# Two heads in natural rows per row group, and the shifted chord of VectorE's exponential on GpSimd

## The chip, the cores and the metric

One core of one Trainium2 chip runs the whole program. The metric is the device time of one execution in microseconds (us), as the median of the runs named. A run more than 1.5% above the fastest of its kernel is called slow and left out of the ratios. Every version was run beside the kernel before, on the same chip in the same session, and the ratio of their fast runs is given with its 95% interval; two changed versions may have run on different chips, so they are compared through these ratios, and differences of their medians are rough. The granted clock is the clock that TensorE was given, as a share of full speed.

## The reference

Attention with 32 heads of width 16 over 2048 positions, then a layer norm with a residual, then a SwiGLU feed-forward block. Cut to what matters:

```python
B, S, D, H, F = 1, 2048, 512, 32, 1792
q, k, v = split(x @ wqkv)                        # 32 heads, Dh = 16
scores = einsum("bhqd,bhkd->bhqk", q, k) * Dh ** -0.5
p = softmax(scores)                              # 32 * 2048 * 2048 exponentials
attn = einsum("bhqk,bhkd->bhqd", p, v)
... attn @ wo, layer norms, residual ...
h = silu(x @ w1) * (x @ w3);  out = h @ w2
```

The exponentials are the load: 1024 score tiles of 128x1024. The rest has to fit beside them.

## The kernel before

The kernel is written as a planner: the program's own scheduler simulates the engines when the program is built and fixes the order of instructions on each engine. The order is then executed as it stands; only semaphores move things in time.

Each score tile goes to ScalarE, which takes a true exponential, or to VectorE, which builds one from integer operations on pairs of tiles:

```python
# VectorE: y = scores as int16 in a fixed-point log2 scale, read from PSUM twice per pair
tensor_scalar(y, ps, G_LO, 32767.0, ALU.max, ALU.min)          # PSUM read, 128x1024, twice
# then on the pair, 128x2048:
tensor_scalar(m, y, 0x7F, 0x3F00, ALU.bitwise_and, ALU.bitwise_or)   # mantissa
tensor_scalar(g, y, -G_LO, 0.0, ALU.add, ALU.max)                    # shifted chord
tensor_tensor(m, y.bitcast(BF16), m.bitcast(BF16), ALU.mult)         # product
tensor_scalar(y, y, 0x7F80, None, ALU.bitwise_and)                   # exponent, in place
```

The results (product, chord, exponent) are three terms that TensorE adds up: each VectorE tile costs three products with V ("PV") in place of one. They live in a few buffers.

```python
NY = 3        # y, and the exponent, which is written in place
NM = 2        # mantissa and product
NG_ = 2       # chord
```

A switched-off path could already give the chord to GpSimd, in another form than VectorE's (the y of this kernel is clamped by the PSUM read, so the max with 0 is not needed):

```python
POOL_G = False
...
# on GpSimd, if POOL_G:
tensor_scalar(g, y, -G_LO, 1.0, ALU.add, ALU.mult)
```

Heads lie at every second group of 16 rows, with a constant row between them that adds the exponent bias; K and Q are brought there by strided moves, and GpSimd prepares the constant rows with seven fills.

## Time and profile before

| | before |
|---|---|
| median of 4 runs | 814.25 us (812.09 to 815.43) |
| span of the profiled run | 812.3 us |
| busy: TensorE, VectorE, ScalarE, GpSimd | 775.6, 775.1, 776.0, 44.1 us |
| first score; first exponential on VectorE | 18.6; 48.9 us |
| last exponential; tail after it | near 795; 17.3 us (cut at 795) |
| tiles on ScalarE and VectorE | 794 and 230 |

The prediction below shows the lines these are from. In a line of the costliest groups, the part before the first bar says what ran, then come busy time in us and the mean ns of one, then the idle time of that engine just before the group and who ended it. "PE ps L..." as releaser is a TensorE instruction of that source line.

### The profile page before, as it was taken

The numbers are of one execution on the slowest core, as the hardware profiler recorded it, in microseconds if no ns is written. First come the engines' busy times: TensorE is split into PE (matmuls) and PEld (weight loads), VectorE is DVE, ScalarE is ACT, GpSimd is POOL, SyncE is SP. The second block draws the span as 40 slices with busy tenths as digits, with TensorE's granted clock in tenths as the row PEclk, the third lists the DMA queues.
The fourth block names the chain that finished last, engine by engine and source line by source line (L and its number), as shares of the span: only waits on it lengthen the run. The fifth ranks groups of instructions, "written<-read, shape, count | busy, mean of one in ns | idle before, by whom it ended". The sixth has DMA issues, their size and how long they took to land.

```text
span 812.3 us, 20816 instructions
## 1 busy us (share of the span) xinstructions
PE 775.6 (95%) x8925; PEld 224.6 (28%) x8925; DVE 775.1 (95%) x1015; ACT 776.0 (96%) x874; POOL 44.1 (5%) x54
## 2 busy tenths in 40 slices
PE   6999999999999999999999999999999999999987
PEld 4332222222222222222222222222222222222222
DVE  8679999999999999999999999999999999999982
ACT  4899999999999999999999999999999999999992
POOL 4500100000000000000001000000000000000000
PEclk9999999999999999999999999999999999999997
DMA  5216333233222313333112434321223432222211
GB/s 182 54 31 149 49 49 52 45 54 40 29 22 41 49 38 43 41 54 47 19 25 28 60 41 54 48 33 40 18 27 55 67 34 34 49 27 22 28 9 31
DMA packets 88783, 36.96 MB, mean 45 GB/s; under 512 B 73193, under 2 KB 85097, under 8 KB 88681
## 3 DMA queue, kind: packets, MB, share of 16 engines
q1 hardware_dynamic: 88680, 35.53, 29.9%
q8 instruction: 72, 1.18, 0.6%
q14 instruction: 31, 0.25, 0.1%
HBM read 22.81 MB, written 2.10 MB: 31 GB/s over the span
## 4 chain that ended last, share of the span: by engine, by line
ACT 50%; PE 24%; DVE 19%; DMA 3%; issue 2%; POOL 1%; SPq 1%; DVEq 0%; POOLq 0%
ACT f_PT L1788 48%; PE ps L1356 9%; PE ps L1742 8%; DVE f_xd L1837 6%; PE ps L2010 6%; ACT f_th L1517 3%; DVE f_xd L1900 3%; DVE f_xd L1909 2%; DVE f_xd L1950 2%; DVE f_xd L1893 2%; DMA f_R<-f_Rrow 2%; DMA f_Rrow<-f_Rc 1%; DVE f_hT L1531 1%; SPq L2058 1%; DVE f_t L1521 1%
## 5 line engine op out<-in xcount | busy, mean ns | idle before, releaser
L1788 ACT ACTIVATE f_PT<-ps 128x1024 bf16<-128x1024 f32 x794 | 746.4, 1091 | 9.9 <-PE ps L1742 9.1
L1742 PE MATMUL ps<-f_QT,f_KT 32*128 32x512 bf16 x2048 | 331.0, 385 | 14.1 <-ACT f_PT L1788 7.1
L1837 DVE TENSOR_SCALAR f_xd<-ps 128x1024 int16<-128x1024 f32 x230 | 278.6, 1211 | 1.6 <-PE ps L1742 1.2
L2010 PE MATMUL ps<-f_PT,f_Vaug 128*17 128x512 bf16 (+1 forms) x1588 | 211.0, 386 | 0.3 <-DVE f_xd L1900 0.3
L2010 PE MATMUL ps<-f_xd,f_Vaug 128*17 128x512 bf16 (+1 forms) x1380 | 191.5, 387 | 3.5 <-DVE f_xd L1950 2.6
L1742 PEld LDWEIGHTS ps<-f_QT,f_KT 32*128 32x128 bf16 x2048 | 83.5, 91 | 328.6 <-ACT f_PT L1788 277.2
L1356 PE MATMUL ps<-f_xnT,f_w 128*32 128x512 bf16 x1792 | 145.0, 384 | 2.5 <-DVE f_hT L1531 0.9
L1900 DVE TENSOR_TENSOR f_xd<-f_xd 128x2048 bf16<-128x2048 bf16 x115 | 142.1, 1235 | 0.0
L1909 DVE TENSOR_SCALAR f_xd<-f_xd 128x2048 int16<-128x2048 int16 x115 | 81.2, 706 | 0.0
L1893 DVE TENSOR_SCALAR f_xd<-f_xd 128x2048 int16<-128x2048 int16 x115 | 79.4, 691 | 0.6 <-PE ps L1356 0.2
L1950 DVE TENSOR_SCALAR f_xd<-f_xd 128x2048 int16<-128x2048 int16 x115 | 79.0, 687 | 0.0
L1356 PE MATMUL ps<-f_w,f_hT 128*32 128x512 bf16 x896 | 74.9, 384 | 0.0
L2010 PEld LDWEIGHTS ps<-f_PT,f_Vaug 128*17 128x17 bf16 (+1 forms) x1588 | 50.6, 92 | 54.4 <-issue 44.7
L2010 PEld LDWEIGHTS ps<-f_xd,f_Vaug 128*17 128x17 bf16 (+1 forms) x1380 | 46.2, 92 | 54.7 <-issue 30.4
L2075 POOL TENSOR_TENSOR f_onorm<-f_U,f_R 128x512 bf16<-128x512 f32 x15 | 21.5, 1431 | 705.2 <-DMA f_R<-f_Rrow 549.3
L1356 PEld LDWEIGHTS ps<-f_xnT,f_w 128*32 128x32 bf16 x1792 | 36.6, 94 | 64.9 <-issue 56.5
L1517 ACT ACTIVATE f_th<-ps 128x512 f32<-128x512 f32 x56 | 38.7, 691 | 0.0
L1531 DVE SCALAR_TENSOR_TENSOR f_hT<-f_t,ps 128x512 bf16<-128x512 bf16 x56 | 37.8, 675 | 0.7 <-PE ps L1356 0.5
L1521 DVE SCALAR_TENSOR_TENSOR f_t<-f_th,ps 128x512 bf16<-128x512 f32 x56 | 37.7, 674 | 0.5 <-ACT f_th L1517 0.3
L1356 PEld LDWEIGHTS ps<-f_w,f_hT 128*32 128x32 bf16 x896 | 18.6, 94 | 26.8 <-issue 22.4
L1356 PE MATMUL ps<-f_wo,f_onorm 128*32 128x512 bf16 x272 | 22.2, 401 | 1.9 <-POOL f_onorm L2075 1.8
L2028 DVE COPY f_U<-ps 128x512 f32<-128x512 f32 x31 | 21.1, 679 | 0.4 <-PE ps L2010 0.3
(80 smaller groups left out, 240.6 us busy)
## 6 DMA issues: line engine op xcount, KB each, us to landing
f_w<-in_B_w_dram SPq DMA_DIRECT2D x112, 128.0 KB, 2.7
f_R<-f_Rrow SPq DMA_DIRECT2D x124, 32.0 KB, 4.4
f_xr<-in_A_x_dram SPq DMA_DIRECT2D x16, 128.0 KB, 3.8
out_dram<-f_xn_sb SPq DMA_DIRECT2D x16, 128.0 KB, 2.5
f_KT<-f_stg SPq DMA_DIRECT2D x31, 64.0 KB, 2.0
f_QT<-f_stg SPq DMA_DIRECT2D x31, 64.0 KB, 2.0
f_U<-f_U SPq DMA_DIRECT2D x60, 32.0 KB, 1.9
f_w<-in_B_w_dram SPq DMA_DIRECT2D x7, 256.0 KB
```

The source lines that it names most:

```text
L1356: ins = e.matmul(bank(bk)[32 * i:32 * i + 32, 0:ncols], make_lhsT(i), rhs_ap, start=start, stop=stop, tile_position=(0, 32 * i))
L1517: q = P.op("act", lambda e: e.activation(th[:, ss, :], bank(bk), ACTF.Tanh, scale=0.5), reads=[("ps", bk)], writes=[("th", ss)], dur=a_cos ...
L1521: q2 = P.op("dve", lambda e: e.scalar_tensor_tensor(t1[:, ss, :], th[:, ss, :], 1.0, bank(bk), ALU.add, ALU.mult), reads=[("th", ss), ("ps ...
L1531: q = P.op("dve", lambda e: e.scalar_tensor_tensor(hT[:, fc, :], t1[:, ss, :], 0.5, bank(bk), ALU.mult, ALU.mult), reads=[("t1", ss), ("ps ...
L1742: ins = e.matmul(bank(b), l_, r_, start=True, stop=True, tile_position=(rp, 0))
L1788: q = P.op("act", lambda e: e.activation(PT[:, s_, :], ps[:, b0 * 512:(b0 + 2) * 512], ACTF.Exp, scale=ASC, bias=ABIAS), reads=[("ps", b0) ...
L1837: q = P.op("dve", lambda e: e.tensor_scalar(dsl[:, ys, 1024 * c:1024 * c + 1024], ps[:, 4 * 512:6 * 512], G_LO, 32767.0, ALU.max, ALU.min) ...
L1893: P.op("dve", lambda e: e.tensor_scalar(dsl[:, NY + m_, 0:n], y, 0x7F, 0x3F00, ALU.bitwise_and, ALU.bitwise_or), reads=YK, writes=[("ds", ...
L1900: q_ = P.op("dve", lambda e: e.tensor_tensor(t_ap.bitcast(BF16), y.bitcast(BF16), t_ap.bitcast(BF16), ALU.mult), reads=YK + [("ds", NY + m ...
L1909: q_ = P.op("dve", lambda e: e.tensor_scalar(g_ap, y, -G_LO, 0.0, ALU.add, ALU.max), reads=YK, writes=[("g", g_, k) for k in range(n // 51 ...
L1950: q_ = P.op("dve", lambda e: e.tensor_scalar(y, y, 0x7F80, None, ALU.bitwise_and), reads=YK, writes=YK, dur=s_cost(n), name="e", lock=True)
L2010: ins = e.matmul(bank(PV)[32 * j:32 * j + (17 if g % 2 == 0 else 32), :], v_, p_, start=s0, stop=s1, tile_position=(0, 32 * j))
```

## The change

The intent is to relieve VectorE twice: to take the chord from it, in pieces of 128x1024 on the idle GpSimd, each released beside a PSUM read because such a read and GpSimd leave each other alone (1.22 and 1.27 us side by side, in the prediction's lines); and to start earlier. Two heads lie in natural rows of a row group, and Q is masked to one of them, so the strided moves and fills vanish. The core of the diff, with cuts:

```diff
-    POOL_G = False
+    NE = 2
+    E_WAIT = 6.0
+    G_POOL = 1.05
+    E_LAG = 0.8
 ...
-                q = ... tensor_scalar(dsl[:, ys, ...], ps[:, 4 * 512:6 * 512], G_LO, 32767.0, ALU.max, ALU.min)
-                beside(q, 1024)
+                before = P.ops["dve"][-1]
+                q = ... tensor_scalar(dsl[:, ys, ...], ps[:, 4 * 512:6 * 512], YB, G_LO, ALU.add, ALU.max)
+                if eq and P.free["pool"] <= P.t + 0.15 and eq[0][1]() is not None:
+                    it = eq.pop(0)
+                    it[2](it[3], before)          # a piece on GpSimd, waiting for `before` alone
 ...
-                q_ = P.op("pool", lambda e: e.tensor_scalar(g_ap, y[:, c0:c0 + w], -G_LO, 1.0, ALU.add, ALU.mult), ...
+            def p_g(c, after, eng="pool"):
+                q_ = P.op(eng, lambda e: e.tensor_scalar(g_ap[:, cs], y[:, cs], -G_LO, 0.0, ALU.add, ALU.max),
+                          ..., dur=G_POOL if eng == "pool" else s_cost(1024), name="g", ...)
 ...
-                q_ = ... tensor_scalar(y, y, 0x7F80, None, ALU.bitwise_and)       # exponent in place
+                q_ = ... tensor_scalar(e_ap, y, 0x7F80, None, ALU.bitwise_and)    # exponent in its own buffer
 ...
+                if eq and P.t - eq[0][0] > E_WAIT and ...:
+                    it[2](it[3], None, "dve")     # a piece that waited 6 us goes back to VectorE
 ...
-        for g in range(1, NG):
-            P.post("pool", lambda g=g: kt_fill(g), ...)        # and stg, pad, pack: strided moves
+                    q = ... tensor_scalar(QT[:, s0, :], QT[:, s1, :], msk[:, 0:1], None, ALU.mult)
+                    q = ... tensor_scalar(QT[:, s1, :], QT[:, s1, :], msk[:, 1:2], None, ALU.mult)
```

## The prediction

> **What bounds the kernel now.** I read the page's busy shares and slices first, then the costliest groups, then busy time by stage, then timelines of a few microseconds in the steady part and around the GpSimd instructions.
>
> ```profile
> PE 775.6 (95%) x8925; PEld 224.6 (28%) x8925; DVE 775.1 (95%) x1015; ACT 776.0 (96%) x874; POOL 44.1 (5%) x54
> ...
> PE   6999999999999999999999999999999999999987
> PEld 4332222222222222222222222222222222222222
> DVE  8679999999999999999999999999999999999982
> ACT  4899999999999999999999999999999999999992
> POOL 4500100000000000000001000000000000000000
> ```
> Three engines are full together from the third slice to the last but one; GpSimd has nothing to do. The 5% that is missing lies at the two ends.
>
> ```profile
> L1788 ACT ACTIVATE f_PT<-ps 128x1024 bf16<-128x1024 f32 x794 | 746.4, 1091 | 9.9 <-PE ps L1742 9.1
> L1742 PE MATMUL ps<-f_QT,f_KT 32*128 32x512 bf16 x2048 | 331.0, 385 | 14.1 <-ACT f_PT L1788 7.1
> L1837 DVE TENSOR_SCALAR f_xd<-ps 128x1024 int16<-128x1024 f32 x230 | 278.6, 1211 | 1.6 <-PE ps L1742 1.2
> ...
> L1900 DVE TENSOR_TENSOR f_xd<-f_xd 128x2048 bf16<-128x2048 bf16 x115 | 142.1, 1235 | 0.0
> L1909 DVE TENSOR_SCALAR f_xd<-f_xd 128x2048 int16<-128x2048 int16 x115 | 81.2, 706 | 0.0
> L1893 DVE TENSOR_SCALAR f_xd<-f_xd 128x2048 int16<-128x2048 int16 x115 | 79.4, 691 | 0.6 <-PE ps L1356 0.2
> ...
> L1950 DVE TENSOR_SCALAR f_xd<-f_xd 128x2048 int16<-128x2048 int16 x115 | 79.0, 687 | 0.0
> ```
> Softmax has 1024 score tiles of 128x1024. ScalarE takes the exponential of 794; VectorE takes 230, in 115 pairs: two PSUM reads, then mantissa, shifted chord (L1909), product, exponent. The schedule is fixed when the program is built and gives a tile to whichever engine is free, so a tile saved on one engine is shared out. The two engines end together, and this balance is what the change moves.
>
> The groups' means contain the pipeline's tail, so for throughput I use start to start distances of the timeline: PSUM read 1.14 us (97.89 to 99.03), product 1.13 (432.14 to 433.27), chain operation 0.60 (96.69 to 97.29), 512-wide PSUM evacuation 0.60, exponential 0.917 (a run of 7 in 6.42 us in the chain of work).
>
> ```profile
> 0.00:18.60 18.60, 11.47 (x104) 8.03 (x104) 14.82 (x39) 7.51 (x11) 8.56 (x20) 1.00 0.63 198
> ...
> 18.60:48.90 30.30, 28.40 (x444) 11.87 (x444) 19.91 (x40) 26.24 (x34) 11.48 (x12) 1.00 0.16 37
> 48.90:795.00 746.10, 724.00 (x8242) 199.65 (x8238) 737.35 (x928) 738.78 (x827) 24.05 (x22) 1.00 0.31 42
> ```
> Columns: stretch, length, then busy us of PE, PEld, DVE, ACT, POOL. The first score comes at 18.6 us. VectorE starts on exponentials only at 48.9 and was idle for 10 of the 30 us before. The last exponential ends near 795; a tail of 17 us follows.
>
> **What the skill says, and whether the trace agrees.**
> "SBUF — State Buffer", section "Who interferes with whom": GpSimd shares a port pair with VectorE as an exclusive lock; a VectorE instruction in a two-port mode, or with two SBUF inputs against a GpSimd read, collides and the later one waits out the earlier; one with at most one SBUF input outside those modes does not. The trace agrees both ways:
>
> ```profile
> 7.82 1.90 POOL L1275 TENSOR_SCALAR f_KT<-f_pat 128x2048 int16<-128x2048 int16 x1
> 7.88 2.30 DVE L1242 TENSOR_SCALAR f_xn_sb<-f_xd,f_mv,f_lnr 128x512 bf16<-128x512 bf16 x2 [0.59 <-POOL f_lnr L1230]
> ...
> 97.89 1.22 DVE L1837 TENSOR_SCALAR f_xd<-ps 128x1024 int16<-128x1024 f32 x1
> ...
> 98.10 1.27 POOL L2075 TENSOR_TENSOR f_onorm<-f_U,f_R 128x512 bf16<-128x512 f32 x1 [62.30 <-DVE f_xd L1909]
> ...
> 432.33 2.75 POOL L2075 TENSOR_TENSOR f_onorm<-f_U,f_R 128x512 bf16<-128x512 f32 x1 [48.12 <-DVE f_xd L1837]
> ```
> Two normalisations behind a GpSimd fill took 2.30 us, where two take 0.70 elsewhere. The PSUM read at 97.89 kept its 1.22 us beside GpSimd, and GpSimd its 1.27; at 432.33, beside the product, GpSimd took 2.75. So PSUM reads are the right hiding place, and the only large one.
> "GPSIMD Engine Reference", section "Engine selection": one-input elementwise work runs at roughly line rate. The seven GpSimd fills agree: 1.90 us for 2048 int16, 1.05 for 1024 f32, so I take 1.05 us for a 1024-wide chord (an estimate: the fills read a broadcast column, not a full tile).
> "TensorEngine Tiling (Array Packing)", section "Key Properties": changing the tiling mode drains the array. At 301 us a step between a score and a column group takes 0.32 us, between two column groups 0.22.
>
> **The change, part by part.**
> 1. Chord to GpSimd. Each pair loses one 0.60 us operation on VectorE: from 2 x 1.14 + 1.13 + 3 x 0.60 = 5.21 us to 4.61, or 2.60 to 2.30 us per tile. GpSimd gets two pieces of 1.05 us per pair, about 125 x 2.1 = 260 us in all, which it has free.
> 2. What the lock takes back. A piece is released by the end of the instruction ahead of the PSUM read. That end comes 0.08 us into the read (1.22 long, 1.14 apart), and a VectorE to GpSimd signal takes 0.09 (5.28 to 5.37 us). So the piece ends about 0.08 + 0.09 + 1.05 = 1.22 us into the read, while the next VectorE instruction is due at 1.14. If that is a chain operation it waits 0.1 us or a little more: per pair up to 0.2, per tile 0.1. I take 2.40 us per tile.
> 3. Natural rows. Gone are the strided moves of K and Q, GpSimd's seven fills, ScalarE's two fills and the second computation of the first K and Q tiles. The constant row becomes the add of the PSUM read (add and max in place of max and min: same cost). Added: two masked copies of Q per Q tile, 15 x 2 x about 0.25 = 7 us of VectorE (estimated from the 0.35 us normalisation of the same width).
> 4. Start-up. K and Q of the first rows are made in 128-column pieces as each transposed tile arrives, and the collision at 7.88 us (1.6 us of the starting chain) goes: first score near 15 us instead of 18.6. Three quarters of V move out of the early part, and K no longer waits for fills and moves, so VectorE's exponentials start near 33 us instead of 48.9. The V evacuations then fall into the steady part: 16 x 0.47 us, half on each engine, 4 us each.
>
> Balance before. ScalarE: 19.1 + 794 x 0.917 (728) + 56 tanh x 0.48 (27) + early evacuations and gaps (21, the remainder) = 795. VectorE: 48.9 + 230 x 2.60 (598) + other work 128 (112 SwiGLU, 31 U, 27 K/Q and 30 output evacuations at 0.60, small ones 8) + gaps 16 (the remainder) = 791. The sums meet, so the model stands.
> Balance after, with n tiles on VectorE. ScalarE: 15 + 17 + 27 + (1024 - n) x 0.917 = 998 - 0.917 n. VectorE: 33 + 2.40 n + 128 + 7 + 4 + 16 = 188 + 2.40 n. Equal at n = 244, ending at 774 us instead of 795. With no lock loss it is n = 252 and 767; with twice the loss n = 237 and 781. The tail stays: 774 + 17 = 791 of span, and the timed runs lie 1 to 2 us above it: 793.
> By parts: with 2.60 us per tile kept, the balance gives n = 230 and 787, so of the 21 us about 8 are the start-up (masks paid) and 13 the offload.
>
> **Rivals.**
> A. TensorE becomes the bound. It is busy 724.0 of 746.1 us, and most of its small gaps are mode switches, not waits. Every tile on VectorE needs three PV products in place of one: 14 more tiles are 14 x 0.22 = 3 us more. Against it: a score of VectorE mostly rides behind one of ScalarE, so a tile fewer on ScalarE saves a visit to score mode (0.64 - 0.22 = 0.42 us), 6 us in all. TensorE's need from first score to last exponential stays near 750 us (28.4 + 724.0 before) in a stretch of 759. It fits barely. If it does not, feed-forward work is left for the tail: 800 to 806.
> B. The lock costs more. If the chord needs 1.3 us on a full tile, or pieces slip behind the product, each PSUM read loses 0.3 us or more, the 0.60 us saved is spent, and only the start-up gain is left: 787 + 17 + 2, about 805. Against: the pieces wait for the instruction ahead of the read, and the schedule sends late ones back to VectorE after 6 us.
> C. The start-up gain is swallowed, because TensorE is already busy 28.4 of 30.3 us there: 4 to 6 us less gain, about 798.
> D. The integer conversion does not saturate. The kernel tests this and would then run its slow path as well: far above 1000 us. I give it 1%.
>
> **Range and chances.** 2% is 16.3 us, so the line is 797.2. The offload alone would not pass it, nor the start-up alone; together they do with 4 us to spare. Rivals A to C each take 5 to 12 us, all from the same side; no lock loss and a shorter tail give back 7 to 10. I say 793, 781 to 806, faster 0.62, same 0.35, slower 0.03.
>
> **What would show it.** Step 1: the mantissa and exponent groups grow to about 120 pairs, the chord group leaves VectorE, GpSimd near 300 us busy, about 240 PSUM reads and 780 exponentials. Step 2: GpSimd pieces near 1.05 us, PSUM reads still 1.21, chain operations behind them 0.1 us longer in the mean. Step 4: first score near 15 us, first VectorE exponential near 33. A: ScalarE shows gaps released by scores, and feed-forward tiles stand after the last exponential. B: chain or product means well above 0.8 and 1.35 us. The prediction is wrong if VectorE's tiles stay near 230, or if ScalarE's last exponential ends after 785.

## The result, and the profile after

The changed kernel takes 974.04 us (median of 4 runs, 967.61 to 985.35) against 814.25; its result is right. One of the four runs was slow (985.35 us at a granted clock of 0.889; the others had 0.907 to 0.909). The ratio is 1.194, with an interval of 1.187 to 1.201. All ratios in this document are the mean time of one kernel's fast runs over that of the other's of the same rounds, so not quite the ratio of the medians that are quoted.

The page of the profiled execution (967.61 us): busy time, and the 40 slices.

```profile
PE 842.5 (87%) x9201; PEld 228.8 (24%) x9201; DVE 810.9 (84%) x1013; ACT 787.4 (82%) x866; POOL 648.7 (67%) x209
...
PE   8898998879889998889989998789888888879887
...
DVE  8888998887869798878989897898987888978872
ACT  6888898878779797778889997798986878868880
POOL 3565785687666696776846775777778975969510
PEclk9979899988879799888989999899987979988999
```

No engine is full any more: three stand at 82 to 87% all along, where they were at 95%. GpSimd, which was to be busy for about 300 us, is busy for 649. The last row is new too: the granted clock of TensorE is below 0.9 in 17 of the 40 slices and 0.907 in the mean, against 0.992 before (its busy time grew from 776 to 843 us with about the same work).

The costliest groups of the kernel after:

```profile
L1817 ACT ACTIVATE f_PT<-ps 128x1024 bf16<-128x1024 f32 x790 | 755.1, 1040 | 146.6 <-PE ps L1771 130.4 <-PE ps L2027 13.6
L1964 POOL TENSOR_SCALAR f_xd<-f_xd 128x1024 int16<-128x1024 int16 x164 | 616.1, 3772 | 249.8 <-DVE f_xd L1922 147.6 <-DVE f_hT L1556 28.2 <-DVE f_xd L1940 21.1
L1868 DVE TENSOR_SCALAR f_xd<-ps 128x1024 int16<-128x1024 f32 x234 | 284.0, 1214 | 32.0 <-PE ps L1771 31.2
...
L2027 PE MATMUL ps<-f_xd,f_Vaug 128*17 128x512 bf16 (+1 forms) x1404 | 206.5, 415 | 72.0 <-POOL f_xd L1964 63.2 <-DVE f_U L2045 3.9 <-DVE f_t L1546 1.8
...
L1929 DVE TENSOR_TENSOR f_xd<-f_xd 128x2048 bf16<-128x2048 bf16 x117 | 152.9, 1307 | 0.0
L1940 DVE TENSOR_SCALAR f_xd<-f_xd 128x2048 int16<-128x2048 int16 x117 | 98.7, 843 | 5.0 <-PE ps L2027 5.0
```

The chain of work that ended last, followed back through the whole execution, as the page of each kernel gives it: first the kernel after, then the kernel before.

```profile
PE 35%; POOL 28%; DVE 21%; issue 7%; ACT 4%; DMA 3%; SPq 1%; DVEq 0%; POOLq 0%
ACT 50%; PE 24%; DVE 19%; DMA 3%; issue 2%; POOL 1%; SPq 1%; DVEq 0%; POOLq 0%
```

GpSimd, which was in 1% of that chain, is now in 28% of it.

The second line of the groups carries the result: one piece on GpSimd takes 3.77 us in the mean, not 1.05. The lines around it show what comes of that. TensorE's products with V stood idle for 63 us until GpSimd had finished (L2027), ScalarE stood idle for 130 us until TensorE made a score (L1771), and VectorE's product and exponent operation grew from 1.24 and 0.69 us to 1.31 and 0.84.

The same kernel by stages; the columns are the stretch, its length, then the busy us of TensorE, its weight loads, VectorE, ScalarE and GpSimd, and the granted clock. The stretches are cut at the first score, the first exponential on VectorE and the last exponential.

```profile
11.60:31.80 20.20, 18.73 (x440) 9.88 (x444) 16.78 (x46) 18.64 (x24) 4.53 (x10) 1.00 0.24 59
31.80:938.00 906.20, 792.92 (x8284) 200.04 (x8284) 778.65 (x928) 760.85 (x831) 639.29 (x183) 0.90 0.23 31
938.00:966.00 28.00, 21.76 (x359) 10.49 (x357) 6.80 (x15) 3.02 (x5) 0.00 (x0) 0.95 0.11 33
```

So the start gained what was hoped for and more: the first score comes at 11.6 us instead of 18.6, VectorE's first exponential at 31.8 instead of 48.9. The steady stretch lost it all many times over: 906 us instead of 746. The tail grew by 11.

A few microseconds of the timeline after (start, length, what ran, and in brackets the idle time before it and who ended that):

```profile
297.11 7.79 POOL L1964 TENSOR_SCALAR f_xd<-f_xd 128x1024 int16<-128x1024 int16 x2
...
299.53 0.69 DVE L1922 TENSOR_SCALAR f_xd<-f_xd 128x2048 int16<-128x2048 int16 x1 [1.72 <-PE ps L2027]
...
301.35 0.40 PE L2027 MATMUL ps<-f_xd,f_Vaug 128*32 128x512 bf16 x4 [1.08 <-POOL f_xd L1964]
...
302.12 4.69 ACT L1817 ACTIVATE f_PT<-ps 128x1024 bf16<-128x1024 f32 x5 [1.04 <-PE ps L1771]
```

This is the chain in small. A first piece runs on GpSimd from 297.11 to about 301; TensorE waits 1.08 us for it; the next score is late by that; ScalarE waits 1.04 us for the score. But look at the second line also: a mantissa operation of VectorE, one of the kind that needs the shared ports, ran in its usual 0.69 us in the middle of the slow piece. So the piece does not keep the ports for its whole length.

### The profile page after: what moved, and what is told of

Its sections match the earlier page's. It is cut to its first block, busy times and chain, and to the rows that moved or that the text cites. A ratio compares the mean times of both kernels' runs of the same rounds, so it can differ in the third digit from the quotient of the medians.

```text
span 965.5 us, 21581 instructions
## 1 busy us (share of the span) xinstructions
PE 842.5 (87%) x9201; PEld 228.8 (24%) x9201; DVE 810.9 (84%) x1013; ACT 787.4 (82%) x866; POOL 648.7 (67%) x209
## 3 DMA queue, kind: packets, MB, share of 16 engines
q8 instruction: 74, 1.21, 0.5%
## 4 chain that ended last, share of the span: by engine, by line
PE 35%; POOL 28%; DVE 21%; issue 7%; ACT 4%; DMA 3%; SPq 1%; DVEq 0%; POOLq 0%
POOL f_xd L1964 26%; PE ps L1328 12%; PE ps L1771 11%; PE ps L2027 10%; DVE f_xd L1868 6%; ACT f_PT L1817 4%; DVE f_xd L1922 3%; DVE f_xd L1929 2%; DVE f_xd L1940 2%; DMA f_R<-f_Rrow 2%; DVE f_xd L1964 2%; DVE f_hT L1556 1%; POOL f_onorm L2092 1%; DVE f_U L2045 1%; DMA f_Rrow<-f_Rc 1%
## 5 line engine op out<-in xcount | busy, mean ns | idle before, releaser
L1817 ACT ACTIVATE f_PT<-ps 128x1024 bf16<-128x1024 f32 x790 | 755.1, 1040 | 146.6 <-PE ps L1771 130.4
L1964 POOL TENSOR_SCALAR f_xd<-f_xd 128x1024 int16<-128x1024 int16 x164 | 616.1, 3772 | 249.8 <-DVE f_xd L1922 147.6
L1771 PE MATMUL ps<-f_QT,f_KT 32*128 32x512 bf16 x2048 | 349.8, 412 | 15.5 <-ACT f_PT L1817 9.3
L1868 DVE TENSOR_SCALAR f_xd<-ps 128x1024 int16<-128x1024 f32 x234 | 284.0, 1214 | 32.0 <-PE ps L1771 31.2
L2027 PE MATMUL ps<-f_xd,f_Vaug 128*17 128x512 bf16 (+1 forms) x1404 | 206.5, 415 | 72.0 <-POOL f_xd L1964 63.2
L2027 PE MATMUL ps<-f_PT,f_Vaug 128*17 128x512 bf16 (+1 forms) x1580 | 227.6, 411 | 22.3 <-POOL f_xd L1964 22.0
L1771 PEld LDWEIGHTS ps<-f_QT,f_KT 32*128 32x128 bf16 x2048 | 81.1, 92 | 353.2 <-ACT f_PT L1817 217.1
L1328 PE MATMUL ps<-f_xnT,f_w 128*32 128x512 bf16 x1792 | 162.1, 421 | 1.7 <-DVE f_t L1546 1.3
L1929 DVE TENSOR_TENSOR f_xd<-f_xd 128x2048 bf16<-128x2048 bf16 x117 | 152.9, 1307 | 0.0
L1922 DVE TENSOR_SCALAR f_xd<-f_xd 128x2048 int16<-128x2048 int16 x117 | 94.6, 809 | 18.8 <-PE ps L2027 18.3
L1940 DVE TENSOR_SCALAR f_xd<-f_xd 128x2048 int16<-128x2048 int16 x117 | 98.7, 843 | 5.0 <-PE ps L2027 5.0
L2027 PEld LDWEIGHTS ps<-f_xd,f_Vaug 128*17 128x17 bf16 (+1 forms) x1404 | 47.8, 94 | 135.4 <-POOL f_xd L1964 85.8
L2027 PEld LDWEIGHTS ps<-f_PT,f_Vaug 128*17 128x17 bf16 (+1 forms) x1580 | 51.2, 93 | 88.2 <-issue 49.0
L1964 DVE TENSOR_SCALAR f_xd<-f_xd 128x1024 int16<-128x1024 int16 x66 | 45.9, 697 | 0.0
```

The lines of the kernel that those rows point to most:

```text
L1328: ins = e.matmul(bank(bk)[32 * i:32 * i + 32, 0:ncols], make_lhsT(i), rhs_ap, start=start, stop=stop, tile_position=(0, 32 * i))
L1771: ins = e.matmul(bank(b), l_, r_, start=True, stop=True, tile_position=(rp, 0))
L1817: q = P.op("act", lambda e: e.activation(PT[:, s_, :], ps[:, b0 * 512:(b0 + 2) * 512], ACTF.Exp, scale=ASC, bias=ABIAS), reads=[("ps", b0) ...
L1868: q = P.op("dve", lambda e: e.tensor_scalar(dsl[:, ys, 1024 * c:1024 * c + 1024], ps[:, 4 * 512:6 * 512], YB, G_LO, ALU.add, ALU.max), rea ...
L1922: P.op("dve", lambda e: e.tensor_scalar(dsl[:, NY + m_, 0:n], y, 0x7F, 0x3F00, ALU.bitwise_and, ALU.bitwise_or), reads=YK, writes=[("ds", ...
L1929: q_ = P.op("dve", lambda e: e.tensor_tensor(t_ap.bitcast(BF16), y.bitcast(BF16), t_ap.bitcast(BF16), ALU.mult), reads=YK + [("ds", NY + m ...
```

## The experiments

Four theories were set up. WAIT: the long pieces deliver late, and TensorE's fixed order waits for them. PORT: the long pieces slow VectorE's own instructions. They concern the loss of 160 us. For the smaller gain that was missing even with short pieces, SLOTS: VectorE waits for buffers that TensorE releases late; and TENSORE: TensorE's work and its order set the end. Some expectations below give these under their own words. The first runs used FORM, LOCK and LAYOUT, which the expectation of experiment 2 explains: FORM is that the piece is slow by its own operations, LOCK that it is slow because VectorE holds the ports.

### 1. What the piece costs by itself

A kernel of its own (it returns zeros) runs batches of six GpSimd instructions on 128x1024, first alone and then beside six VectorE instructions. The block below sums its batches up; it is not code.

```diff
+ add, max       int16      # L184; also bf16 L190, f32 L191, broadcast column L192
+ add, mult 1.0  int16      # L185
+ mult 1.0, add  int16      # L186, the pair of the fills
+ add alone      int16      # L187
+ max alone      int16      # L188
+ max, add       int16      # L189
+ add, mult on GpSimd beside: PSUM reads (L204), exponent operations (L206), products (L208)
+ add, max  on GpSimd beside: PSUM reads (L210), exponent operations (L212), products (L214)
```

> Not the task: a bench that writes zeros on purpose. Six GpSimd operations of 128x1024 in each stage. Alone, int16: A add+max, B add+multiply, C multiply+add, D add, E max, F max+add; then add+max in bf16 (G), f32 (H), with a broadcast column (I). FORM expects A 3.6 us each and B, C 1.0 to 1.1 with nobody else running; LOCK expects A about 1.05 too. Then with VectorE running: add+multiply beside PSUM reads (J), beside 2048-wide int16 operations (K), beside the two-input product (L); the same three with add+max (M, N, O). The lock as the skill has it: J undisturbed at 1.05, K and L queue one behind the other; N and O make VectorE wait 3.6 us for each piece.

Groups of this kernel:

```profile
L184 POOL TENSOR_SCALAR g<-y 128x1024 int16<-128x1024 int16 x6 | 21.6, 3624 | 11.3 <-DVE ps L170 11.3
L187 POOL TENSOR_SCALAR g<-y 128x1024 int16<-128x1024 int16 x6 | 16.4, 2768 | 0.1
L188 POOL TENSOR_SCALAR g<-y 128x1024 int16<-128x1024 int16 x6 | 16.4, 2764 | 0.1
L206 DVE TENSOR_SCALAR d<-d 128x2048 int16<-128x2048 int16 x6 | 7.9, 1384 | 0.0
L210 DVE TENSOR_SCALAR d<-ps 128x1024 int16<-128x1024 f32 x6 | 6.9, 1217 | 0.0
L186 POOL TENSOR_SCALAR g<-y 128x1024 int16<-128x1024 int16 x6 | 6.3, 1045 | 0.4
L185 POOL TENSOR_SCALAR g<-y 128x1024 int16<-128x1024 int16 x6 | 6.3, 1044 | 0.4
L212 DVE TENSOR_SCALAR d<-d 128x2048 int16<-128x2048 int16 x6 | 6.2, 1100 | 0.0
```

The cost goes with the pair of operations: 3.62 us for add and max (and the same, to 2 ns, for bf16, f32, max and add, and a broadcast column), 2.77 for add alone or max alone, 1.04 for add and multiply, 1.05 for multiply and add. VectorE is not needed for the slowness, so LOCK is out; and a max in second place is not what makes it, as the expectation of FORM had it, since a single add is slow too. Every fast pair here multiplies by 1.0: another factor, or a multiplication alone, was not tried, and why the pairs differ no run shows. Nor does a PSUM read of VectorE mind either form (1217 ns, as ever). The exponent operation, which takes about 0.69 us in the kernels, needs 1.10 in the mean beside slow pieces and 1.38 beside fast ones that it queues with. Six slow pieces beside exponent operations last 22.6 us (21.6 alone) and the six exponent operations were through in 6.2, so they slipped in between: they were slowed, not locked out. The product took 1.49 us beside slow pieces and 1.92 beside fast ones, against about 1.24 in the kernels; and a fast piece beside products took 1.94.

### 2. The change with a fast pair; and with no chord on GpSimd at all

Since the PSUM read of the changed kernel already clamps at the chord's offset, the max with 0 changes nothing, and multiplying by 1.0 gives the same result. The comparison with the reference passed, but it passed in experiment 6 too, with half of a contraction left out; so the equality rests on the clamp, not on the comparison.

```diff
-  tensor_scalar(g_ap[:, cs], y[:, cs], -G_LO, 0.0, ALU.add, ALU.max)
+  v1, op1 = (1.0, ALU.mult) if eng == "pool" else (0.0, ALU.max)
+  tensor_scalar(g_ap[:, cs], y[:, cs], -G_LO, v1, ALU.add, op1)
```

> Only the GpSimd chord changes its form: add then multiply by 1.0 in place of add then max with 0 (the max is redundant, since the PSUM read has already clamped at 352; the result stays right). The static order is unchanged. Theory FORM (GpSimd needs 3.63 us for a piece because of the max as second operation, whatever VectorE does): pieces near 1.05 us, waits of TensorE for GpSimd gone, 787 to 803 us. Theory LOCK (the piece is slow because VectorE holds the shared port): pieces stay above 3 us and the time near 970. Theory LAYOUT (natural rows and start-up are to blame): pieces faster, time still above 900.

Measured: 824.15 us (819.47 to 826.13), ratio 1.011 (1.006 to 1.016). That is 150 us less than the changed kernel for two words of one instruction, so the pair of operations is the cause of the large loss. Yet it is 31 us above the prediction, and above the 787 to 803 expected.

```profile
L1965 POOL TENSOR_SCALAR f_xd<-f_xd 128x1024 int16<-128x1024 int16 x164 | 176.7, 1078 | 488.5 <-DVE f_xd L1922 260.1 <-DVE f_xd L1940 45.3 <-DVE f_hT L1556 41.1
...
L1929 DVE TENSOR_TENSOR f_xd<-f_xd 128x2048 bf16<-128x2048 bf16 x117 | 149.4, 1277 | 0.0
L1922 DVE TENSOR_SCALAR f_xd<-f_xd 128x2048 int16<-128x2048 int16 x117 | 84.1, 719 | 11.1 <-PE ps L2028 10.4
...
L1965 DVE TENSOR_SCALAR f_xd<-f_xd 128x1024 int16<-128x1024 int16 x66 | 30.0, 457 | 0.0
```

The piece now takes 1.08 us, within 3% of the prediction's 1.05. But the plan sends 66 of 230 pieces back to VectorE, and VectorE waits 10.4 us before the mantissa operation until TensorE (L2028, the products with V) has released a buffer.

The other half of the change alone, with every chord on VectorE:

```diff
-            by_pool = nc_ == 2 and sl["rr"] > E_LAST
+            by_pool = False
```

> The changed kernel with every chord on VectorE, as one 2048-wide operation: natural rows and start-up alone. FORM and LOCK: no slow GpSimd piece is left, so 800 to 810 us (my balance said 805). LAYOUT: above 900.

Measured: 816.79 us (815.68 to 818.31), ratio 1.002 (0.997 to 1.007). The prediction had about 805 for this, the expectation 800 to 810; LAYOUT (above 900) is out. Here too the wait for buffers stands (mantissa, product and chord of VectorE):

```profile
L1922 DVE TENSOR_SCALAR f_xd<-f_xd 128x2048 int16<-128x2048 int16 (+1 forms) x111 | 78.9, 711 | 16.3 <-PE ps L2027 15.8
...
L1929 DVE TENSOR_TENSOR f_xd<-f_xd 128x2048 bf16<-128x2048 bf16 (+1 forms) x111 | 134.8, 1214 | 0.0
...
L1956 DVE TENSOR_SCALAR f_xd<-f_xd 128x2048 int16<-128x2048 int16 (+1 forms) x111 | 76.6, 690 | 0.0
```

Before, the same wait was 0.6 us in all. VectorE takes 221 tiles instead of 230, although it starts 17 us earlier.

### 3. The plan told the true duration

If the late results were the whole trouble, a schedule that reckons with 3.7 us should cure it.

```diff
-    G_POOL = 1.05
+    G_POOL = 3.7
```

> The changed kernel with add and max on GpSimd as it is, but the program's own schedule is told that a piece lasts 3.7 us in place of 1.05. FORM, with the loss coming from a static order built on a wrong duration: TensorE hardly waits for GpSimd, fewer pieces go to GpSimd (about 100 to 150), 800 to 830 us. If instead a slow piece harms by itself (holds the port against VectorE): still above 880 and chain operations on VectorE well above 0.8 us.

Measured: 890.79 us (887.30 to 896.19), ratio 1.093. The plan puts 84 pieces on GpSimd and TensorE's waits for it shrink to 2.3 us; 83 us of the 160 go. But VectorE gets only 177 tiles, is 71% busy, and waits 57 us for ScalarE, which takes 847.

```profile
L1964 POOL TENSOR_SCALAR f_xd<-f_xd 128x1024 int16<-128x1024 int16 x84 | 307.1, 3656 | 462.8 <-DVE f_xd L1922 279.1 <-DVE f_U L2045 50.8 <-DVE f_hT L1556 37.9
...
L1940 DVE TENSOR_SCALAR f_xd<-f_xd 128x2048 int16<-128x2048 int16 (+1 forms) x89 | 61.9, 695 | 0.1
```

Neither half of the expectation came true: the time is far above 830, yet VectorE's chain operations kept about 0.70 us beside the 84 slow pieces. So slowed chain operations do not explain the loss that is left here; the plan is the likelier cause, beside a granted clock of 0.942. The plan's simulation holds VectorE's mantissa, product and exponent until a piece has ended (`P.port`), which these lines do not bear out; that this is why VectorE gets so few tiles is argued, not shown.

### 4. Slow pieces that nobody waits for

All chords are on VectorE, as in the second half of experiment 2, and 162 add-and-max pieces run on a scratch tile beside PSUM reads; no instruction reads their result.

```diff
+                if by[0] % 4 != 3 and P.free["pool"] <= P.t + 0.15:
+                    P.op("pool", lambda e: e.tensor_scalar(scr, scr, -G_LO, 0.0, ALU.add, ALU.max), ..., extra=[before])
+                by[0] += 1
```

> The changed kernel with all chords on VectorE (817 us) plus about 165 add+max pieces of 128x1024 on GpSimd, released as the real ones are, on a scratch tile that nobody reads. WAIT (the slow piece costs because TensorE's fixed order waits for its result): 817 to 830, chain operations on VectorE a few tenths of a us longer where they overlap (the bench said 0.3 to 0.4 us each). PORT (the slow piece costs by holding the port against VectorE): above 880.

Measured: 893.84 us (892.36 to 898.59), ratio 1.098 (1.093 to 1.102): 77 us more than without the bystander.

```profile
L1872 POOL TENSOR_SCALAR f_scr<-f_scr 128x1024 int16<-128x1024 int16 x162 | 609.9, 3765 | 193.5 <-DVE f_xd L1929 138.3 <-DVE f_xd L1963 10.6 <-DVE f_KT L1440 10.2
...
L1875 DVE TENSOR_SCALAR f_xd<-ps 128x1024 int16<-128x1024 f32 x221 | 267.6, 1211 | 1.1 <-PE ps L1774 1.0
L1936 DVE TENSOR_TENSOR f_xd<-f_xd 128x2048 bf16<-128x2048 bf16 (+1 forms) x111 | 151.6, 1366 | 0.0
L1963 DVE TENSOR_SCALAR f_xd<-f_xd 128x2048 int16<-128x2048 int16 (+1 forms) x111 | 109.4, 985 | 0.0
```

This shows that PORT alone can cost as much as 77 us, against what I had held more likely: no result is waited for. It does not show that half of the changed kernel's loss came this way. Here VectorE also has all the chords, its busy time rose by 88 us, and GpSimd is in 1% of the chain that ended last; in the changed kernel VectorE's busy time is 53 us above that of the fast-pair version (810.9 against 758.1), and GpSimd is in 28% of that chain. Both theories hold there, in shares that no run took apart. The PSUM read kept its 1.21 us; the product went from 1.21 to 1.37, the chord operation from 0.69 to 0.99, and VectorE's busy time from 758 to 846 us. The pieces are three times as long as the PSUM read they are hidden beside, so they reach into everything that follows it. PORT works by some tenths of a microsecond on each operation that needs the shared ports, not by whole pieces.

The same with fast pieces:

```diff
-  tensor_scalar(scr, scr, -G_LO, 0.0, ALU.add, ALU.max)
+  tensor_scalar(scr, scr, -G_LO, 1.0, ALU.add, ALU.mult)
```

> The version without any chord on GpSimd, with 162 pieces of the fast pair (add, then times 1.0) on a scratch tile that nobody reads, each released beside a PSUM read as in the changed kernel. If a fast piece hidden there costs VectorE nothing: within 0.7% of that version, 812 to 822 us, VectorE busy near 758 us. If the product and the mantissa and exponent operations wait for it now and then: VectorE busy 770 to 785 us, product mean above 1.26 us, time 823 to 832.

Measured: 822.78 us (818.61 to 823.94), ratio 1.008 (1.005 to 1.012), against 1.002 without pieces: about 5 us, but the two intervals overlap. The time lies between the two expected bands. VectorE's busy time rose by 7 us, to 765.5, just below the upper band; the product took 1.24 us (1.21 without). Hiding beside PSUM reads is cheap when the piece fits, and by VectorE's busy time not quite free.

### 5. The offload alone, on the kernel before

```diff
-    POOL_G = False
+    POOL_G = True
```

> The kernel before with its own switch for the chord on GpSimd turned on (that code uses add and multiply): the offload alone, old rows, old start-up. My prediction's balance gave 800 for it. TENSORE: VectorE takes a few tiles more and the last exponential ends 5 to 8 us earlier, but the tail grows by as much: 810 to 820. A GpSimd piece near 1.05 us either way.

Measured: 828.87 us (827.95 to 829.68), ratio 1.017 (1.014 to 1.020). That is above the 810 to 820 expected. With the fast pair (1.085 us in the mean, 236 pieces) and none of the new start, the older offload path loses time: VectorE's busy share falls from 95 to 90%, and its exponent operation waits 10.1 us for GpSimd, which in this path must be done first because the exponent is written in place. Freed VectorE time did not turn into speed here either.

### 6. Less and more work for TensorE

To test TENSORE, half of the SwiGLU contraction was taken away (about 49 us of TensorE work) from three kernels: before, the fast-pair version, and the version with no chord on GpSimd. Their outputs are wrong, which doesn't matter for the times.

```diff
-                for c in range(DC):
+                for c in range(2):
```

> The kernel before with half of the contraction of the two SwiGLU projections left out (wrong on purpose): 56 x 2 x 2 groups of four matmuls x 0.22 us = 49 us of TensorE work gone, the other engines as they were. Theory TENSORE (TensorE is the bound in the kernels with a fast chord, so what VectorE and ScalarE save is only left over as TensorE work behind the last exponential) sees three engines in balance here and expects little: 808 to 814. Theory SLOTS (VectorE is held back by waits for its buffers and by new work, TensorE does not matter) expects the same.

> The same cut of TensorE work in the changed kernel with add and multiply on GpSimd (824 us uncut). TENSORE: the offload's gain appears once TensorE has room: 798 to 811, a drop of 12 us or more, and the tail after the last exponential shrinks from 26 us to about 16. SLOTS: 817 to 824.

> The same cut in the changed kernel with all chords on VectorE (817 us uncut). TENSORE as the only bound: below 808, since its first score comes 7 us earlier than in the kernel before. SLOTS: 811 to 817, the start-up gain being eaten by VectorE's waits for free buffers (16 us), Q masks (10 us) and V evacuations (7 us).

Measured: 823.61 (822.16 to 830.43), 818.06 (811.16 to 825.95) and 826.59 us (825.30 to 829.88), ratios 1.012, 1.000 and 1.014. The first and the third became slower by about 10 us and lie outside all expected bands. The second is different: its three fast runs have a median of 814.73 us, between its two bands, and its ratio fell from 1.011 to 1.000, about 9 us, though its granted clock was only 0.956 to 0.968. The stages of the third show what spoils the test (columns as above; the last two lines lie within the second):

```profile
50.00:700.00 650.00, 614.32 (x6708) 169.67 (x6700) 626.06 (x813) 646.27 (x729) 21.28 (x17) 1.00 0.30 41
700.00:800.00 100.00, 95.72 (x612) 18.03 (x611) 85.53 (x103) 88.49 (x92) 2.61 (x2) 0.59 0.16 9
...
700.00:710.00 10.00, 8.06 (x71) 2.16 (x71) 10.00 (x14) 10.00 (x12) 0.00 (x0) 1.00 0.08 15
...
720.00:740.00 20.00, 19.96 (x124) 3.62 (x120) 14.84 (x21) 16.14 (x17) 0.00 (x0) 0.50 0.15 6
```

From 700 to 800 us the granted clock was 0.59, where it had been 1.00, and what was left took longer. Just before it fell, TensorE was busy for only 8.06 of 10 us, waiting for ScalarE; that these gaps brought the clock down is inferred from the order in time. The profiled run of the second was slow and is not used. As a test of TENSORE this is spoilt for the first and the third; the second speaks for TENSORE in part.

The reverse, one chunk of the contraction computed twice (25 us more work planned, of which 13 to 15 us show in busy time), on before and on the fast-pair version (both edits also add one wait on VectorE in a small check of the row sums, not shown here):

```diff
-                for c in range(DC):
+                for k_, c in enumerate([0, 1, 2, 3, 3]):
```

> The kernel before with one chunk of the SwiGLU contraction done twice (wrong on purpose): 56 x 2 x 0.22 = 25 us more of TensorE work, nothing else[...]. TENSORE as a bound already in the kernel before: 830 to 842, the extra work standing behind the last exponential. TensorE with slack: 813 to 820.

> The same 25 us added to the changed kernel with add and multiply on GpSimd (824 us). TENSORE: 840 to 852, all of it in the tail while the last exponential stays near 790. Slack: 824 to 830.

Measured: 826.47 (825.50 to 828.40) and 826.02 us (822.11 to 827.58): 12 us more for the kernel before, between its two bands, but only 2 more for the fast-pair version, inside the band for slack; the granted clock was 0.988 to 0.994. So more work did not cost that version anything clear of noise. But the plan, and with it the order, changed as well, and in experiments 7 and 8 other plans of the same work moved the time by 6 to 12 us, so this is no proof that it had room on TensorE.

### 7. Other tuning constants with the fast pair

The changed constants, gathered in two lines:

```diff
-    PVQ, E_WAIT, E_LAG, VB0, VBS, G_POOL, D_LEFT = 28, 6.0, 0.8, 24, 5, 1.05, 10
+    PVQ, E_WAIT, E_LAG, VB0, VBS, G_POOL, D_LEFT = 26, 9.0, 0.5, 12, 8, 1.1, 6
-    DG, PV wait = 0.24, 2
+    DG, PV wait = 0.22, 1.2
```

> Add and multiply on GpSimd with the schedule's constants retuned (a piece planned at 1.1 us, up to 9 us of patience before VectorE takes it back, less margin, more room for feed-forward work before PV): the same work in another order, 220 pieces on GpSimd in place of 164. If the order is what stands in the way: 798 to 810, below the kernel before. If TensorE's amount of work is: 815 or more.

Measured: 812.31 us (809.65 to 814.14), ratio 0.996 (0.993 to 0.999). That is 12 us less than the fast-pair version took, and between the two expected bands. The total work is the same, but 222 pieces run on GpSimd in place of 164 and 12 on VectorE in place of 66, so order and split changed together; it shows how little a difference of some microseconds between two plans means. The wait for the mantissa buffer stayed (9.0 us).

A softer test of TENSORE on this version, with three of four chunks:

```diff
-                for c in range(DC):
+                for c in range(3):
```

> The retuned version with three of the four chunks of the SwiGLU contraction (wrong on purpose): about 25 us less work for TensorE, half of what was taken away before, in the hope that its clock stays up. If TensorE is the limit: 785 to 800 us, with the last exponential no later than 790 and a short tail. If ScalarE and VectorE are: 806 to 813, the last exponential still near 789. A granted clock under 0.97 leaves it open.

Measured: 805.17 us (801.59 to 806.59), ratio 0.988 (0.985 to 0.992). It fell between the two expected bands, at a granted clock of 0.973 to 0.980, just above the limit I had set. Against the version with all four chunks (0.996) it is about 7 us faster, so TensorE's work matters somewhat here; how much can't be told from it.

### 8. A third buffer

SLOTS, put to the test in four kernels:

```diff
-    NM = 2
+    NM = 3
-    NE = 2
+    NE = 3
```

(in the kernel before, which has no buffer of its own for the exponent, NM and NG_).

With the fast pair:

> The changed kernel with the fast pair, with three buffers in place of two for the mantissas and for the exponent results. If VectorE is held up by buffers that TensorE releases late: its waits before the mantissa operation (11 us) vanish, more tiles go to it (near 239 in place of 234), and the time falls to 808 to 816. If the order of TensorE's work and its total set the end: 820 to 826, the waits turning up elsewhere.

Measured: 811.47 us median, ratio 0.998 (0.993 to 1.004); four of six runs lay at 810.1 to 811.6, one fast one at 820.8, and one slow one at 822.69. That is 13 us below the fast-pair version (11 by the ratios), as SLOTS had it; the wait before the mantissa operation fell from 10.4 us to 0.8:

```profile
L1922 DVE TENSOR_SCALAR f_xd<-f_xd 128x2048 int16<-128x2048 int16 x120 | 87.3, 728 | 1.4 <-PE ps L2028 0.8
```

With the other tuning constants:

> The retuned version with the same two extra buffers. Buffers: below 808 us. TensorE's work as the limit: 810 to 815.

Measured: 818.25 us (812.17 to 824.07), ratio 1.004 (0.999 to 1.009): neither band. The buffer wait went (0.5 us), but ScalarE's waits for scores rose from 16.5 to 19.2 us and TensorE's matmuls after 780 us from 331 to 441. The extra buffers change the plan and so the order everywhere; this one was worse.

With no chord on GpSimd:

> All chords on VectorE, natural rows and the new start, with the third mantissa and exponent buffer: the start-up gain without GpSimd and without the wait for buffers. If that wait (16 us before the mantissa operation) is what swallowed the start-up gain: the wait goes, about 229 tiles on VectorE, last exponential near 788, 804 to 810 us. If the tail or TensorE swallow it anyway: 814 to 819.

Measured: 800.24 us (799.90 to 802.38), ratio 0.981 (0.979 to 0.984). This is the fastest version of all, below even the band expected (804 to 810); at 1.9% under the kernel before it stays just short of the 2% that counts as faster here. Its busy page and two groups:

```profile
PE 767.9 (96%) x9181; PEld 227.2 (28%) x9181; DVE 772.3 (97%) x1047; ACT 771.4 (97%) x873; POOL 34.4 (4%) x45
...
L1956 DVE TENSOR_SCALAR f_xd<-f_xd 128x2048 int16<-128x2048 int16 (+1 forms) x115 | 79.6, 693 | 0.0
L1922 DVE TENSOR_SCALAR f_xd<-f_xd 128x2048 int16<-128x2048 int16 (+1 forms) x115 | 79.4, 691 | 0.2
```

Its stages, from the first exponential of VectorE to the last exponential, and the tail:

```profile
31.80:780.30 748.50, 727.15 (x8448) 202.41 (x8446) 742.11 (x964) 746.63 (x839) 25.02 (x19) 1.00 0.28 37
780.30:798.70 18.40, 12.65 (x189) 5.97 (x179) 4.69 (x13) 1.79 (x3) 0.00 (x0) 0.97 0.11 36
```

And those of the version with the fast pair and the third buffer:

```profile
31.80:782.50 750.70, 721.93 (x8338) 200.56 (x8336) 732.26 (x936) 738.81 (x827) 210.27 (x194) 1.00 0.28 37
782.50:808.40 25.90, 20.29 (x331) 9.64 (x325) 5.76 (x14) 1.79 (x3) 0.00 (x0) 0.94 0.12 35
```

Side by side these two show what the fast offload did in this plan: the stretch of exponentials is no shorter (750.7 against 748.5 us), although VectorE takes 239 tiles instead of 229; all three engines are idler in it; and TensorE has 331 matmuls left for the tail instead of 189.

The control, the third buffer in the kernel before:

> The kernel before with a third buffer for the mantissas and for the shifted chords. Its mantissa operation waits only 0.6 us in all, so if the buffers helped the natural-row version only because its order of work made them scarce: no change, 811 to 817 us. If a third buffer is worth something in any order of work: 800 to 808 us, and the gain of the version with the new start would not be the start's.

Measured: 815.02 us (813.68 to 817.03), ratio 0.998 (0.996 to 1.000). The buffer does nothing for the kernel before. So the gain to 800 us belongs to the natural rows and the new start, which came together and were not taken apart; the want of buffers had hidden it.

## Why the prediction was wrong

The prediction was 793 us with a range up to 806; it is 974. Point by point:

**Step 1, "so I take 1.05 us for a 1024-wide chord".** This is the step that failed: a term of the sum that was mis-sized by 3.5. The piece takes 3.62 us alone and 3.77 in the kernel. The estimate was read from the fills, and the text itself named one difference, the broadcast column, which turned out not to matter. The one that did matter was in the diff: the fills multiply and add, the chord adds and takes a maximum. Of the 181 us between prediction and result, 150 go with two words of that instruction (experiment 2). How they divide stays open. Slow pieces that nobody waits for cost 77 us by way of VectorE's slowed operations (experiment 4), but on a VectorE that also had the chords. In the changed kernel VectorE's busy time is 53 us above that of the fast-pair version, TensorE waits 85 us for late chords (63 in one group, 22 in another), and its granted clock is 0.907 in place of 0.990; these overlap, and no run took one alone.

**Step 2, the lock.** The sum allowed 0.1 us per tile. With fast pieces the product grew by 42 ns over the kernel before, the mantissa by 28 and the exponent by 20, in all 0.09 us per pair, or 0.045 per tile, over all pairs (164 of 230 pieces were on GpSimd): cheaper than predicted. With the slow ones it was 72, 118 and 156 ns, 0.17 per tile, and that understates it, as late VectorE results delay others.

**Step 3, natural rows.** Masks were put at 7 us of VectorE; they are two groups of 5.3 and 5.2 us with fast pieces, 10.5 in all. Small.

**Step 4, the start.** Right, and better than said: first score at 11.6 us (15 predicted), VectorE's first exponential at 31.8 (33 predicted).

**The balance.** It said 805 us for the start alone. Measured it was 817, and 800 with a third buffer, with 229 tiles on VectorE (230 predicted) and the last exponential at 780 (787 predicted). So the model of two engines that end together fits that version, but it assumed that VectorE never waits for a buffer. That had been true of the kernel before (0.6 us) and was carried over unexamined to an order of work in which it was not: 16 us. Two of its numbers are not derived: ScalarE's 21 us of early evacuations and gaps become 17 without a word, and the line of 797.2 us should be 798.0 for a median of 814.25.

**The offload.** It was to bring 12 to 13 us. With the right pair, and buffers enough, it costs 11 (811.5 against 800.2; 14 by the ratios) with these constants; the other set of constants was tried only with the offload. About 5 us of fast-piece interference were seen, not clear of noise, in a kernel that is short of buffers (experiment 4); 59 of the pieces, a quarter, go back to VectorE and take 25 us there; and more is left for the tail. How the 11 us divide stays open. So does the share of TENSORE: with less work for TensorE two fast-pair versions became 7 and 9 us faster, with more work one lost nothing clear of noise, and the other light tests were spoilt by the clock.

**The rivals.** B was the right kind ("If the chord needs 1.3 us on a full tile") but was costed as a lost saving, with an end at 805. It did not ask what happens to the engine that waits for the chord. A shows in the longer tail (26 us with 17 predicted). C was what the version without the offload looked like, but for another cause: not TensorE's early stretch but buffers. D did not happen. Of the prediction's own signs of being wrong, VectorE's tiles near 230 (234) and a last exponential after 785 (938) both came.

## What to carry to other kernels

A duration for a planned instruction should come from the same operation pair on that engine, not from one of the same shape: when the diff changes the operations of an instruction, measure that instruction by itself first. A freed engine is worth only what the buffers and the fixed order of its neighbours let it use; look for a wait on a buffer in every version, and before believing in an offload, run the rest of the change without it. Here the best version of those run was the change minus its headline, plus one more buffer: 800.24 us.

## What the Trainium skill lacked or had wrong

- "GPSIMD Engine Reference", section "Engine selection": one-input elementwise work as roughly line-rate. True here of add with multiply (1.04 us for 128x1024) and multiply with add (1.05), not of add with max (3.62), nor of a single add (2.77) or max (2.76). The page has no difference between such operations.
- "GPSIMD Engine Reference", section "Elementwise — side-by-side cycle accounting": "For k ≤ 2 the body is RD/WR-port-bound at 1.03 cyc/elem". At the 1.2 GHz of that section, 1024 elements give an estimate of 0.88 us, which is near the 1.04 of the fast pairs; the add-and-max pair, also of two operations, took 3.54 ns per element (3.62 us). Adding a multiplication to a single add made it faster (2.77 to 1.04 us).
- "SBUF — State Buffer", section "Who interferes with whom": a collision "fully blocks" for the whole instruction. The fast pieces come near that (six pieces and six exponent operations took 8.76 us together, where one after the other they would take an estimated 9.9, from 6 x 1.04 and 6 x 0.60). The slow pieces do not: six exponent operations finished in 6.2 us beside pieces of 3.6 us each. That a PSUM read is free of it held throughout (1.21 us).
- "TensorE: Matmul & The Clock Gate", section "HAM oscillation — how this bites in real kernels": it warns of idle gaps longer than about 3.4 us. What these runs add is a case in which taking work from TensorE made the program longer: 826.6 instead of 816.8 us, the clock at 0.59 from 700 to 800 us. In the 14 us before it fell the longest gap between matmuls in the trace was 0.54 us.
